# Attention and MLP for one decoded token: the load of wq divided between two DMA queues, 16 partitions on ScalarE's and 112 on SyncE's

## The chip, the cores and the metric

The kernel runs on one core of a Trainium2 chip. The metric is the device time of one execution in microseconds (us). The chip's core has a TensorE for matrix products (PE in the profile), a VectorE (DVE), a ScalarE (ACT), a GpSimd (POOL) and a SyncE (SP). Data come from HBM through 16 DMA engines, which are handed their work through queues: one that SyncE issues to (q1 in the profile) and one that ScalarE issues to (q10).

## What is computed

One token x of 512 numbers goes through a layernorm, attention over a cache of 16,384 keys and values with 8 key heads and 32 query heads, a projection with a residual, and then a second block: layernorm, a mixer, layernorm, an MLP with 1,792 hidden units. Cut to what matters:

```python
q = layernorm(x) @ wq                      # wq: 512 x 4096, bf16, 4 MB
scores = q . k_cache * 128 ** -0.5         # k_cache: 8 heads x 16384 x 128
o = softmax(scores) . v_cache              # v_cache: the same size
h = x + o @ wo                             # wo: 4096 x 512
# block B on layernorm(h): with a sequence of one, the mixer's four
# shifted parts are all zero, so that x1 is its input
out = h + x1 + gelu(layernorm(x1) @ w3) @ w4
```

The keys are 32 MB and the values 32 MB; wq, wo, w3 and w4 add 12 MB (wq and wo 4 MB each, w3 and w4 1.8 MB each). Each byte is used once.

## The kernel before

The kernel is written out by hand. A small class `Program` keeps a list of operations for each engine, in the order in which the Python calls are made. Each operation names the keys that it reads (`r`) and writes (`w`), and the class adds a wait on a semaphore wherever an operation needs one from another engine. An engine takes its own list strictly in order; so does SyncE, whose list is almost only DMA issues. A wait stops everything behind it on that engine.

**Loads.** `load` (L224-225) issues one DMA, by SyncE if nothing else is said. The order of issue is: x4, the small input of 1 KB, by ScalarE (L325); wq by SyncE (L326), 128 partitions of 32 KB each into the buffer `vb`; the first half and the second half of the first pair of key heads (L327-328), each 128 partitions of 32 KB, into the two halves of `kb`. The DMAs after that are issued when a buffer comes free: `vb` takes the values of pair 0 (8 MB, 64 KB in each partition, L241) when the matmuls on wq are done with it, and so on. The four pairs of heads follow each other; keys of the next pair are issued while the values of this one are still moving. At the end wo, w3 and w4 are loaded in pieces into the buffer of the keys.

**Head of the kernel.** VectorE makes an identity and from it `quarter` (L337). TensorE spreads x4 over all partitions with it (L339), VectorE makes sums, variance and inverse root of the layernorm (L272-L320) and writes `xn` (L345), then some constants and masks (L350-L370). TensorE multiplies `xn` with wq (L378, 32 matmuls), VectorE lays the queries out (L382, L388). The values of pair 0 are issued when the last of the matmuls of L378 is done.

**Loop over pairs.** For each half of the keys VectorE transposes (L397), TensorE makes scores (L405); then softmax (L416-L433), values (L448), gathering (L459-L465). After the loop come wo (L509), the second layernorm, w3 (L543), gelu (L555), w4 (L571) and the output (L577, L580).

Buffers that a load is to overwrite are guarded by keys: wq and the values of every pair share the key `"v"`, so that the load of the values waits for the readers of wq.

Of the kernel before, what the change touches and what calls it, by code (L numbers as in the profile page):

```python
# [110 lines left out]
HQ = 32  # L111
HKV = 8
SK = 16384
DH = 128
REP = HQ // HKV
FM = 1792
NCH = D // 128
FQ = FM // 4
NHC = FM // 128
WO = ((0, 24), (24, 32))  # L120
W3 = ((0, 4),)
W4 = ((0, 10), (10, 13), (13, 14))
# [10 lines left out]
def bass_sequential_preLN__gqa_block_cached__mixer_s_mlp__decode_kernel(  # L133
# [13 lines left out]
    with ExitStack() as ctx:  # L147
# [31 lines left out]
        xn = sb("xn", [128, NCH], BF16)  # L179
# [24 lines left out]
        hT = sb("hT", [128, NCH, 32], FP32)  # L204
        hcol = sb("hcol", [128, NHC, 32], BF16)
        fin = sb("fin", [64, 256], BF16)
        kb_all = sb("kb", [128, 256 * DH], BF16)
        kb = [kb_all[:, i * 128 * DH:(i + 1) * 128 * DH] for i in range(2)]
        vb = sb("vb", [128, 256 * DH], BF16)
        kt = sb("kt", [128, 128 * DH], BF16)  # L210
        wq_sb, wo_sb = vb, kb[0]
        w3_sb = kb[1][:, 0:NCH * FM].rearrange("p (k f) -> p k f", k=NCH)
        w4_sb = kb[1][:, NCH * FM:2 * NCH * FM].rearrange("p (m c) -> p m c", m=NHC)

# [9 lines left out]
        def load(name, dst, src, key, by="SP", also=()):  # L224
            P.op(by, lambda e: e.dma_start(dst, src), w=[key, *also], dma=name)  # L225

        def pair_rows(src, j):
            return src[0, 2 * j:2 * j + 2].rearrange("g (u t) d -> (g u) (t d)", u=64)

        def load_keys(j, y):  # L230
            n = 128 * DH
            if j in WHOLE:
                if y:
                    load("k0", kb_all[:, :], pair_rows(A_k_cache, j), ("r", 0, 0),
                         also=[("r", h, i) for h in range(2) for i in range(RPARTS)])
                return
            load(f"k{y}", kb[y][:, :], pair_rows(A_k_cache, j)[:, y * n:(y + 1) * n], ("r", y, 0),
                 also=[("r", y, i) for i in range(1, RPARTS)])

        def load_values(j):  # L240
            load("v", vb[:, :], pair_rows(A_v_cache, j), "v")  # L241


        def dve(fn, r=(), w=(), bank=()):
            return P.op("DVE", fn, r, w, bank)

        def act(fn, r=(), w=(), bank=()):
            return P.op("ACT", fn, r, w, bank)
# [4 lines left out]
        def pe(fn, r=(), w=(), bank=()):  # L253
            return P.op("PE", fn, r, w, bank)

        def piece(cuts, m):
            return [lo <= m < hi for lo, hi in cuts].index(True)

        def spin(n, out=1):

            for _ in range(n):
                pe(lambda e: e.matmul(O_ps[out][:, :], qb[:, 0, 0, 0:128], kt[:, 0:512], start=True, stop=True),  # L262
                   r=["qb", ("kt", 0)], w=[("O", out)], bank=[("O", out)])

        def copies(col, n):

            return col.to_broadcast([col.shape[0], n])
# [40 lines left out]
        def inverse_root(i, n, by):  # L308
# [7 lines left out]
            for k in range(3):  # L316
# [5 lines left out]
                   r=[(S, 8 + n), (T, n)], w=[key])  # L322


        load("x4", x4[:, :], A_x[0, 0:1, :].rearrange("o (q j) -> (o q) j", q=4), "x4", "ACT")  # L325
        load("wq", wq_sb[:, 0:NCH * HQ * DH], A_wq.rearrange("(p k) c -> p (k c)", k=NCH), "v")  # L326
        load_keys(0, 0)  # L327
        load_keys(0, 1)

# [8 lines left out]
            r=["ident_f"], w=["quarter"])  # L338
        pe(lambda e: e.matmul(O_ps[0][:, 0:128], quarter[:, :, :].rearrange("p q u -> p (q u)"), x4[:, :],  # L339
                              start=True, stop=True), r=["quarter", "x4"], w=[("O", 0)], bank=[("O", 0)])  # L340
# [6 lines left out]
            r=["hT", (("st", 0), 0), (("st", 0), 6)], w=["xn"])  # L347
# [9 lines left out]
            r=["ident_f"], w=["row32"])  # L357
        dve(lambda e: e.tensor_reduce(maskdd[:, :], ident_f[:, :].rearrange("p (n d) -> p d n", d=4), AX.X, ALU.add),
            r=["ident_f"], w=["maskdd"])
# [14 lines left out]
        for j, (row, key) in enumerate(rows):  # L374
            for k in range(NCH):
                for g in range(2):
                    at = k * HQ * DH + (2 * j + g) * REP * DH
                    pe(lambda e, row=row, k=k, g=g, at=at: e.matmul(  # L378
                        row[64 * g:64 * g + 64, :], copies(xn[:, k:k + 1], 64), wq_sb[:, at:at + REP * DH],
                        start=(k == 0), stop=(k == NCH - 1)), r=["xn", "v"], w=[key], bank=[key])  # L380
            for b in range(2):
                dve(lambda e, j=j, b=b, row=row: e.transpose(  # L382
                    qcol[:, j, 2 * REP * b:2 * REP * (b + 1), :].rearrange("p m u -> p (m u)"),
                    row.rearrange("p (h b i e) -> p b e h i", b=2, i=32, e=2)[:, b, :, :, :]),
                    r=[key], w=["qcol"], bank=[key])
        for a in range(4):
            lo, hi, at = 32 * a, 32 * a + 32, QPAD + 32 * a
# [65 lines left out]
        def gather(j):  # L453

            O, key = O_ps[j % 2], ("O", j % 2)
            for c in range(4):
# [10 lines left out]
               r=["od", "zo"], w=["A"], bank=["A"])  # L467

        load_values(0)
        for j in range(PAIRS):  # L470
            for y in range(2):
                transpose_keys(y, range(8))
                scores(j, y, range(8))
                if j < PAIRS - 1:
                    load_keys(j + 1, y)
            softmax(j)
            if j == PAIRS - 1:
                spin(SPINS[2], 0)
            values(j)
            if j == PAIRS - 1:  # L480
                spin(SPINS[3], 0)
            gather(j)
            if j < PAIRS - 1:
                load_values(j + 1)
        act(lambda e: e.activation(scr[0:1, 1:2], mean4[0:1, 0:1], ACTF.Gelu_apprx_tanh), r=["mean4"], w=["scr"])
        for n, (lo, hi) in enumerate(WO):
            load(f"wo{n}", wo_sb[:, lo * D:hi * D], A_wo.rearrange("(p r) c -> p (r c)", p=128)[:, lo * D:hi * D],
# [5 lines left out]
        for n, (lo, hi) in enumerate(W4):  # L493
# [7 lines left out]
            r=["o_m"], w=["o_f"])  # L501
# [3 lines left out]
        for r_ in range(32):  # L505
            q = r_ % 4
            if r_ == WO[1][0]:
                spin(SPINS[5])
            pe(lambda e, r_=r_, q=q: e.matmul(O_ps[0][32 * q:32 * q + 32, :], copies(o_b[:, r_:r_ + 1], 32),  # L509
                                              wo_sb[:, r_ * D:(r_ + 1) * D], start=(r_ < 4), stop=(r_ >= 28)),  # L510
               r=["o_b", ("r", 0, piece(WO, r_))], w=[("O", 0)], bank=[("O", 0)])
        h_ps, hkey = s_ps[:, 1, :], ("s", 1)
        pe(lambda e: e.matmul(h_ps[:, 0:128], quarter[:, :, :].rearrange("p q u -> p (q u)"), x4[:, :],
                              start=True, stop=False, skip_group_check=True),
           r=["quarter", "x4"], w=[hkey], bank=[hkey])
        dve(lambda e: e.tensor_copy(osum[:, :], O_ps[0][:, :]), r=[("O", 0)], w=["osum"], bank=[("O", 0)])  # L516
        for i in range(2):
            for n in range(2):
                pe(lambda e, i=i, n=n: e.matmul(
                    h2_ps[64 + 32 * i:96 + 32 * i, 128 * n:128 * n + 128], quarter[:, 2 * i + n, :], x4[:, :],  # L520
                    start=(n == 0), stop=False, skip_group_check=True), r=["quarter", "x4"], w=["h2"], bank=["h2"])
        spin(SPINS[6])
        for q in range(4):
            pe(lambda e, q=q: e.matmul(h_ps[32 * q:32 * q + 32, 0:128], copies(row32[:, 0:1], 32),
                                       osum[:, q * 128:(q + 1) * 128], start=False, stop=True, skip_group_check=True),
               r=["osum", "row32"], w=[hkey], bank=[hkey])
# [3 lines left out]
        for i in range(2):  # L530
            pe(lambda e, i=i: e.matmul(
                h2_ps[64 + 32 * i:96 + 32 * i, 0:256], copies(row32[:, 0:1], 32), osum[:, 256 * i:256 * i + 256],
                start=False, stop=True, skip_group_check=True), r=["osum", "row32"], w=["h2"], bank=["h2"])
        spin(SPINS[8])
        act(lambda e: e.activation(hc[:, :, :], hT[:, :, :], ACTF.Identity, bias=s[:, 0:1], scale=1.0),
            r=["hT", (S, 0)], w=["hc"])
        act(lambda e: e.activation(hr2[64:128, :], h2_ps[64:128, 0:256], ACTF.Identity, bias=0.0, scale=1.0),
            r=["h2"], w=["hr2"], bank=["h2"])


        for k in range(NCH):
            for q in range(4):
                pe(lambda e, k=k, q=q: e.matmul(s_ps[32 * q:32 * q + 32, 0, 0:FQ], hc[:, k, :],  # L543
                                                w3_sb[:, k, q * FQ:(q + 1) * FQ], start=(k == 0), stop=(k == NCH - 1)),
                   r=["hc", ("r", 1, piece(W3, k))], w=[("s", 0)], bank=[("s", 0)])
# [7 lines left out]
        for n in range(2):  # L553
            lo, hi = n * NHC // 2, (n + 1) * NHC // 2
            act(lambda e, lo=lo, hi=hi: e.activation(  # L555
                hg[:, :].rearrange("p (i m) -> p i m", m=NHC)[:, :, lo:hi],
                s_ps[:, 0, 0:FQ].rearrange("p (i m) -> p i m", m=NHC)[:, :, lo:hi],
                ACTF.Gelu_apprx_tanh, scale=s[:, 7:8]), r=[("s", 0), (S, 7)], w=[("hg", n)], bank=[("s", 0)])
            dve(lambda e, lo=lo, hi=hi: e.transpose(
                hcol[:, lo:hi, :].rearrange("p m u -> p (m u)"),  # L560
                hg[:, :].rearrange("p (i m) -> p m i", m=NHC)[:, lo:hi, :]), r=[("hg", n)], w=[("hcol", n)])
        dve(lambda e: e.tensor_tensor(xsum[64:128, :], hr2[64:128, :], xs2[64:128, :], ALU.add),
            r=["hr2", "xs2"], w=["xsum"])

        turns = {m: m % 2 if m < W4[0][1] else 0 for m in range(NHC)}
        for m in range(NHC):
            t = turns[m]
            same = [k for k in turns if turns[k] == t]
            bank, key = ((n_ps, "n"), (B_ps, "B"))[t]
            for o in range(2):  # L570
                pe(lambda e, m=m, o=o, lo=64 * t + 32 * o, bank=bank, same=same: e.matmul(  # L571
                    bank[lo:lo + 32, 0:256], hcol[:, m, :], w4_sb[:, m, o * 256:(o + 1) * 256],
                    start=(m == same[0]), stop=(m == same[-1])),
                   r=[("hcol", 2 * m // NHC), ("r", 1, 2 + piece(W4, m))], w=[key], bank=[("B" if t else "mn")])
        dve(lambda e: e.tensor_tensor(part[:, :], xsum[64:128, :], B_ps[64:128, 0:256], ALU.add),
            r=["B", "xsum"], w=["part"], bank=["B"])
        dve(lambda e: e.tensor_tensor(fin[:, :], part[:, :], n_ps[0:64, 0:256], ALU.add),  # L577
            r=["n", "part"], w=["fin"], bank=["mn"])
        for o, by in enumerate(("SP", "ACT")):
            P.op(by, lambda e, o=o: e.dma_start(out[0, 0:1, 256 * o:256 * o + 256], fin[32 * o:32 * o + 1, :]),  # L580
                 r=["fin"], w=[("out", o)], dma=f"out{o}")
# [32 lines left out]
```

## Time and profile before

| | us |
|---|---|
| median of 3 runs | 191.53 (191.33 to 191.57) |
| the profiled execution's own time | 191.19 |
| its span, from first to last instruction on the core | 189.9 |
| what lies around the span | 1.3 |
| PE, DVE, ACT, POOL busy | 122.6, 115.8, 9.4, 7.0 |
| moved through q1 (SyncE's queue) | 79.17 MB in 2,594 packets |
| moved through q10 (ScalarE's queue) | 10 packets, some 2 KB |

How to read it: the profile gives the busy time of each engine, a picture of the span in 40 slices, the DMA queues, the chain of work that ended last, and groups of instructions by line of the kernel. L378 is line 378 of the listing above. "SPq" and "ACTq" are DMA issues by SyncE and ScalarE: their time is that of the issue, not of the transfer. A packet is one piece of a DMA that one of the 16 DMA engines moves; the trace has start, duration, size and queue of each. The page's times are microseconds from the start of the span.

### The profile page before, as it was taken

The page shows a single profiled execution, that of the slowest core. Times are in us where ns is not written, and L with a number is a line of the kernel's source. Part 1 is how long each engine was busy: PE and PEld are TensorE (multiplying, and loading weights), DVE is VectorE, ACT ScalarE, POOL GpSimd, SP SyncE. Part 2 cuts the span into 40 slices and gives each one's busy share as a digit, 9 for nine tenths or more (in the row PEclk, how much of TensorE's full clock was granted, in tenths as well). Part 3 has the DMA queues.
Part 4 walks back from the last instruction along what each step waited for, and adds up shares of the span by engine and source line. Part 5 has one row for each costly group of instructions (what it writes and reads, how often), then busy time and mean ns, then how long its engine had stood idle before and what let it go on. Part 6 is the DMA issues. An engine that isn't in the chain of part 4 may idle for free.

```text
span 189.9 us, 1730 instructions
## 1 busy us (share of the span) xinstructions
PE 122.6 (65%) x726; PEld 45.9 (24%) x726; DVE 115.8 (61%) x176; ACT 9.4 (5%) x16; POOL 7.0 (4%) x15
## 2 busy tenths in 40 slices
PE   0129099693085004999449599944929998779893
PEld 0114033221032001342123222212313422334231
DVE  7755597993502007999450999935079897514274
ACT  3000000002000000000110000011000000500011
POOL 7100000000000000000000000000000000000032
PEclk9999969999558555799956999996575999999999
DMA  6999999999999999997999999999999999989992
GB/s 221 442 442 442 442 442 444 442 442 431 442 442 442 428 442 442 442 442 342 442 435 428 456 442 414 390 442 414 442 442 442 469 431 414 442 368 409 433 408 84
DMA packets 2610, 79.26 MB, mean 417 GB/s; under 512 B 298, under 2 KB 428, under 8 KB 556
## 3 DMA queue, kind: packets, MB, share of 16 engines
q1 hardware_dynamic: 2594, 79.17, 97.2%
q8 instruction: 5, 0.08, 0.2%
q14 instruction: 1, 0.01, 0.0%
q10 hardware_dynamic: 10, 0.00, 0.0%
HBM read 79.17 MB, written 0.00 MB: 417 GB/s over the span
## 4 chain that ended last, share of the span: by engine, by line
DMA 61%; DVE 31%; PE 4%; issue 1%; SPq 1%; ACT 1%; ACTq 0%
DMA kb<-in_A_k_cache_dram 46%; DVE kt L397 28%; DMA kb<-in_B_w_dram 14%; PE O_ps L448 3%; DVE pt L433 1%; SPq L225 1%; DVE mx L416 1%; ACT p_sb L429 1%; DVE od L462 1%; PE s_ps L405 1%; PE mn_ps L571 0%; DVE fin L577 0%; PE mn_ps L423 0%; PE mn_ps L419 0%; DVE od L459 0%
## 5 line engine op out<-in xcount | busy, mean ns | idle before, releaser
L405 PE MATMUL s_ps<-kt,qb 128*128 128x512 bf16 x256 | 69.5, 411 | 24.4 <-DVE kt L397 21.6
L397 DVE STREAM_TRANSPOSE kt<-kb 128x1024 int32<-128x1024 int32 x64 | 72.8, 1206 | 16.7 <-DMA kb<-in_A_k_cache_dram 16.7
L405 PEld LDWEIGHTS s_ps<-kt,qb 128*128 128x128 bf16 x256 | 22.8, 102 | 70.2 <-DVE kt L397 45.7
L448 PE MATMUL O_ps<-vb,pt 128*32 128x512 bf16 x256 | 21.9, 517 | 10.7 <-DMA vb<-in_A_v_cache_dram 6.3
L459 DVE TENSOR_SCALAR od<-O_ps,rowc 128x128 f32<-128x128 f32 x4 | 1.4, 350 | 28.0 <-PE O_ps L448 28.0
L448 PEld LDWEIGHTS O_ps<-vb,pt 128*32 128x32 bf16 x256 | 8.9, 125 | 22.5 <-issue 11.0
L433 DVE STREAM_TRANSPOSE pt<-p_sb 64x1024 bf16<-64x1024 bf16 x8 | 9.9, 1240 | 5.4 <-ACT p_sb L429 5.3
L262 PE MATMUL O_ps<-kt,qb 128*128 128x512 bf16 x52 | 12.9, 380 | 0.0
L429 ACT ACTIVATE p_sb<-s_ps,bias 128x1024 bf16<-128x1024 f32 x4 | 4.5, 1114 | 156.5 <-DVE nmh L425 156.5
L416 DVE TENSOR_REDUCE mx<-s_ps 128x1 f32<-128x1024 f32 x4 | 4.9, 1225 | 4.5 <-PE s_ps L405 4.5
L378 PE MATMUL O_ps<-vb,xn 128*64 128x512 bf16 x16 | 3.6, 631 | 5.8 <-DMA vb<-in_A_wq_dram 5.8
L315 POOL TENSOR_SCALAR st<-st 128x1 f32<-128x1 f32 x1 | 0.2, 244 | 177.5 <-DVE st L300 177.5
L262 PEld LDWEIGHTS O_ps<-kt,qb 128*128 128x128 bf16 x52 | 4.5, 99 | 6.0 <-issue 1.8
L465 PE MATMUL A_ps<-od,zz 128*128 128x128 f32 x8 | 2.0, 326 | 5.1 <-DVE od L462 5.1
L437 PE MATMUL A_ps<-acc,zz 128*128 128x1 f32 x8 | 1.6, 271 | 5.3 <-ACT p_sb L429 5.3
L462 DVE SCALAR_TENSOR_TENSOR od<-O_ps,rowc,od 128x128 f32<-128x128 f32 x12 | 4.2, 351 | 0.4
L419 PE MATMUL mn_ps<-ident_f,mx 128*1 128x128 f32 x8 | 1.5, 271 | 4.4 <-DVE mx L416 4.4
L337 DVE CAST quarter<-ident_f 4x128 bf16<-4x128 f32 x1 | 3.9, 3904 | 0.6 <-POOL ident_f L332 0.6
L339 PE MATMUL O_ps<-x,quarter 4*128 4x128 bf16 x1 | 0.3, 282 | 5.7 <-DVE quarter L337 5.7
L382 DVE STREAM_TRANSPOSE qcol<-O_ps 128x256 f32<-128x256 f32 x4 | 1.6, 428 | 3.9 <-PE O_ps L378 3.9
L378 PEld LDWEIGHTS O_ps<-vb,xn 128*64 128x64 bf16 x16 | 1.4, 167 | 7.2 <-DVE zz L367 5.9
L516 DVE COPY osum<-O_ps 128x512 f32<-128x512 f32 x1 | 0.7, 691 | 3.7 <-PE O_ps L509 3.7
(87 smaller groups left out, 50.9 us busy)
## 6 DMA issues: line engine op xcount, KB each, us to landing
kb<-in_A_k_cache_dram SPq DMA_DIRECT2D x6, 4096.0 KB, 23.5
vb<-in_A_wq_dram SPq DMA_DIRECT2D x1, 4096.0 KB, 12.2
kb<-in_A_wo_dram SPq DMA_DIRECT2D x1, 3072.0 KB, 27.2
kb<-in_B_w_dram SPq DMA_DIRECT2D x1, 1792.0 KB, 24.2
kb<-in_B_w_dram SPq DMA_DIRECT2D x1, 1280.0 KB, 27.0
kb<-in_A_wo_dram SPq DMA_DIRECT2D x1, 1024.0 KB, 29.2
kb<-in_B_w_dram SPq DMA_DIRECT2D x1, 384.0 KB, 27.4
kb<-in_B_w_dram SPq DMA_DIRECT2D x1, 128.0 KB, 27.3
```

The costliest lines, as they stand in the source:

```text
L225: P.op(by, lambda e: e.dma_start(dst, src), w=[key, *also], dma=name)
L262: pe(lambda e: e.matmul(O_ps[out][:, :], qb[:, 0, 0, 0:128], kt[:, 0:512], start=True, stop=True), r=["qb", ("kt", 0)], w=[("O", out)], ba ...
L337: dve(lambda e: e.tensor_copy(quarter[:, :, :], ident_f[0:4, 0:4].unsqueeze(2).to_broadcast([4, 4, 32])), r=["ident_f"], w=["quarter"])
L378: pe(lambda e, row=row, k=k, g=g, at=at: e.matmul(row[64 * g:64 * g + 64, :], copies(xn[:, k:k + 1], 64), wq_sb[:, at:at + REP * DH], star ...
L397: dve(lambda e, view=view: e.transpose(view(kt), view(kb[y])), r=[("r", y, n) for n in range(RPARTS)], w=[("kt", t)])
L405: pe(lambda e, n=n, c=c: e.matmul(s_ps[:, y, :], qb[:, n, j, QPAD - 4 * c:QW - 4 * c], ktv[:, n // 2, n % 2, :, 8 * c:8 * c + 8, :], start ...
L416: dve(lambda e: e.tensor_reduce(mx[:, :], s_all, AX.X, ALU.max), r=[("s", 0), ("s", 1)], w=["mx"], **both)
L429: act(lambda e: e.activation(p_sb[:, :], s_all, ACTF.Exp, bias=bias[:, 0:1], scale=float(SCALE), accum_out=acc[:, :]), r=[("s", 0), ("s", ...
L433: dve(lambda e, g=g: e.transpose(pt[64 * g:64 * g + 64, :, :, g, :], p_sb[64 * g:64 * g + 64, :]), r=["p"], w=["pt"])
L448: pe(lambda e, q=q, ct=ct, xl=xl, ch=ch: e.matmul(O_ps[j % 2][32 * ct:32 * ct + 32, :], pt[:, xl, ch, :, :].rearrange("p g u -> p (g u)"), ...
L462: dve(lambda e, block=block, c=c: e.scalar_tensor_tensor(od[:, :], block, rowc[:, c:c + 1], od[:, :], ALU.mult, ALU.add), r=[key, "rowc", ...
L465: pe(lambda e: e.matmul(A_ps[:, 0:128], zo[:, 96 - 32 * j:224 - 32 * j], od[:, :], start=False, stop=(j == PAIRS - 1), skip_group_check=True),
```

## The change

wq is loaded by two DMAs in place of one. Partitions 0 to 15 (512 KB) are issued by ScalarE as its first DMA, partitions 16 to 127 (3,584 KB) by SyncE as its first. x4 becomes ScalarE's second DMA; before, it was its only one until the output. The two parts have keys and semaphores of their own, `("wq", 0)` and `("wq", 1)`; the matmuls of L378 wait for both, and the loads of values name both among what they overwrite. Nothing else is touched; all lines behind the first edit move down by one to three.

```diff
+WQ = ((0, 16), (16, 128))
...
         def load_values(j):
-            load("v", vb[:, :], pair_rows(A_v_cache, j), "v")
+            load("v", vb[:, :], pair_rows(A_v_cache, j), "v", also=[("wq", 0), ("wq", 1)])
...
+        wq_in = A_wq.rearrange("(p k) c -> p (k c)", k=NCH)
+        for n, (lo, hi) in enumerate(WQ):
+            load(f"wq{n}", wq_sb[lo:hi, 0:NCH * HQ * DH], wq_in[lo:hi, :], ("wq", n), ("ACT", "SP")[n])
         load("x4", x4[:, :], A_x[0, 0:1, :].rearrange("o (q j) -> (o q) j", q=4), "x4", "ACT")
-        load("wq", wq_sb[:, 0:NCH * HQ * DH], A_wq.rearrange("(p k) c -> p (k c)", k=NCH), "v")
         load_keys(0, 0)
         load_keys(0, 1)
...
-                        start=(k == 0), stop=(k == NCH - 1)), r=["xn", "v"], w=[key], bank=[key])
+                        start=(k == 0), stop=(k == NCH - 1)), r=["xn", ("wq", 0), ("wq", 1)], w=[key], bank=[key])
```

## Prediction

> **What bounds the kernel now.** I read first the page's slices, then its DMA queues, then the chain of work that ended last, in order of time. The slices and queues:
>
> ```profile
> DMA  6999999999999999997999999999999999989992
> GB/s 221 442 442 442 442 442 444 442 442 431 442 442 442 428 442 442 442 442 342 442 435 428 456 442 414 390 442 414 442 442 442 469 431 414 442 368 409 433 408 84
> ...
> q1 hardware_dynamic: 2594, 79.17, 97.2%
> ...
> q10 hardware_dynamic: 10, 0.00, 0.0%
> ```
>
> The reader is to see that the 16 DMA engines are busy from the second slice to the 39th, and that one queue, SyncE's, holds them 97.2% of the span. The trace's packets say it more sharply. One packet is one partition's row; a row of 32 KB takes an engine 1.213 us in the steady stream (27.0 GB/s), the next starts where it ends, and from 2.6 to 186 us the engines together lack only 0.37 us (the mean over the 16) of being always in a packet of data. No engine takes over another's rows: each DMA of 128 partitions ends with 16 signs of completion, one per engine, and an engine that is late stays late to the end. In the last DMA (the end of w4) ten engines are done at 186.0 to 186.5 us and six at 187.2 to 187.8 us; those six have had one fetch of instructions each (page: q8 five, q14 one) among their rows.
>
> The chain, first and last pieces:
>
> ```profile
> 1.64 31.49 DMA kb<-in_A_k_cache_dram
> ...
> 42.34 30.01 DMA kb<-in_A_k_cache_dram
> ...
> 72.38 18.15 DVE kt L397 x16
> ...
> 160.02 27.42 DMA kb<-in_B_w_dram
> 187.44 0.04 issue
> 187.48 0.64 PE mn_ps L571 x8
> ```
>
> The DVE pieces in it lie beside full queues; the stream of rows runs on under them. So what makes the stream later in its first 13 us makes the end later by as much, on the slowest engine, and what makes it earlier makes the end earlier. Whatever delays only an engine's computing in the head costs something only if it outlasts its cover. The head:
>
> ```profile
> 0.71 0.56 ACTq L225 DMA_DIRECT2D x<-in_A_x_dram  x1
> 0.72 0.40 SPq L225 DMA_DIRECT2D vb<-in_A_wq_dram  x1
> ...
> 1.31 1.28 ACT L351 ACT_TABLE_LOAD   x1 [1.31 <-PEq L599]
> ...
> 5.66 0.28 PE L339 MATMUL O_ps<-x,quarter 4*128 4x128 bf16 x1 [5.66 <-DVE quarter L337]
> ...
> 10.06 0.29 DVE L345 TENSOR_SCALAR xn<-hT,st 128x4 bf16<-128x4 f32 x1
> ...
> 13.09 3.62 PE L378 MATMUL O_ps<-vb,xn 128*64 128x512 bf16 x16 [5.84 <-DMA vb<-in_A_wq_dram]
> ...
> 18.88 0.33 SPq L225 DMA_DIRECT2D vb<-in_A_v_cache_dram  x1
> ```
>
> Both queues are issued to at the same moment. By the packets, x4's first row starts at 1.67 us, wq's first rows at 1.74 to 2.04 us on fifteen engines and at 2.60 us on the last. These first rows take 1.54 to 2.19 us, not 1.21, and end at 3.57 to 4.14 us; from there the pace is steady, and wq is complete at 12.96 us.
>
> **The change part by part.**
>
> Bytes: the same. x4 (4 partitions) shows as 4 rows and 4 signs on q10, one row to an engine; I take it that 16 partitions give each engine one row and 112 give it seven, so 8 rows of wq per engine as before, 8 x 1.213 = 9.7 us.
>
> Change-over between queues: this is the term that I think decides. Before, an engine draws all rows of wq from one queue; after, from two. The trace shows what a foreign packet costs an engine's stream. Five fetches on q8 (16 KB, 0.61 us at 27.0 GB/s) took 0.95 to 1.07 us, 0.34 to 0.46 too much, and the row behind each of them took 0.48 to 0.55 us too long (2.90 for 2.42, 1.76 for 1.21, 0.79 for 0.31). The one late fetch on q14 took its normal 0.31, and the row behind it 0.61 too long. No data packet ran beside them on the same engine: the row begins where the fetch ends. Going out and back thus cost 0.83 to 0.96 us beyond the bytes for the five and 0.61 for the one; I take 0.93, near the middle of the five. ScalarE's row of wq is one such packet in SyncE's stream, on all 16 engines, the late six included, so it goes whole to the end. Lower bound: -0.57 us, the spread of the first rows' ends, if the change-over is free and all engines start like the first. Upper bound by change-overs: the completion sign behind the row is one more packet of ScalarE's, so twice 0.93 = 1.9 us. On the four engines with x4 it is up to 3.7 us (x4's row and sign are two more), from which up to 1.3 us is hidden where an engine isn't one of the six. I keep one change out and back, since q1's own signs (9 ns each) stretch no row.
>
> x4: before, its rows land at 1.7 us and are needed at 5.66, when `quarter` is ready. After, they stand behind a 32 KB row in the same queue. With one row of each queue ahead they land near 4.1 + 0.5 + 1.2 = 5.8 us, or 0.2 late. At worst they come behind all rows of wq, at 13.9. Then `xn` comes 4.7 us later (5.66 to 10.35) at 18.6 us, the queries' matmuls (13.09 to 18.81, 5.7) end at 24.3, and the values of pair 0 are issued at 24.4 us instead of 18.88. The two key halves keep q1 filled until 31.8 us on the first engine; so 7.4 us of cover remain. VectorE's key transposes (from 22.68) would begin some 3.4 us late, at 26.1 behind the queries' layout (1.8 us after the matmuls), and reach their second half 2.1 us late; the next keys, issued at 42.34, have cover until values 0 end at 51.2. Cost of x4: 0.
>
> ScalarE's table load at 1.31 waits behind one more issue (0.40 to 0.56); ScalarE is next needed at 46.1 us. Cost 0. SyncE's list has the same issues, one of them smaller. The second wait of L378 ends with the stream: wq comes at 12.96 + 0.93 = 13.9, and values 0 are issued at 19.8, with 12 us of cover. Cost 0 beyond the 0.93.
>
> Sum: 191.19 + 0.93 = 192.12 us for an execution like the profiled one. That one lies 0.34 below the median of the runs, 191.53; on the median **192.46 us**. All times below are on the median.
>
> **The rivals.**
>
> *The narrow part is slow to land* (slower, more). [...] Chance 0.26.
> [...]
>
> *The head starts better* (faster). Mechanism: 16 rows are described quicker than 128, so ScalarE's DMA fills the engine that now starts at 2.60 us as early as the others, and SyncE's rows stand ready behind. The last engine gains at most 2.60 - 1.74 = 0.86; I price it at the spread of the first rows' ends, 4.14 - 3.57 = 0.57: 190.96 us. It decides if a change-over between two queues that are both filled beforehand costs less than 0.57. For it: the fetches that I price from come unannounced into a running stream. Against it: the row that suffers is SyncE's, whose queue was full. Chance 0.22.
>
> *Nothing* (the rows of two queues follow like those of one, the start as before; SyncE's issue of wq, 0.40 us, is no shorter on the path, since the first rows come 0.6 us behind its end): 191.5. For it: q1's own DMAs follow each other without a gap. Against it: the stretched rows behind the fetches. Chance 0.15.
> [...]
>
> **How the numbers follow.** Forecast 0.37, its own range 191.8 (one change-over, 0.3) to 193.4 (two out and back); narrow part 0.26; better head 0.22; nothing 0.15. About 0.2%, or 0.38 us, is what a measurement of this kernel can tell from no change. Slower: 0.35 of the forecast and 0.26 = 0.61. Same: 0.15, 0.02 of the forecast, 0.04 of the better head = 0.21. Faster: 0.18. The range reaches from 190.9, below the better head's price, to 196.2, the narrow part with change-overs; outside are meetings of the 112 rows (about 0.12) and a gain above 0.6 us (about 0.06).
>
> **What would show it.** Right: first rows of q1 behind a q10 row longer by about 0.5 us, wq complete near 13.9, all later landings late by the same 0.9. [...] If the head is better, first rows end before 4.0 us on all engines and wq lands before 12.9. If q10's rows take 1.2 us and q1's rows aren't stretched, my price of the change-over is wrong. An L339 past 8 us with L378 waiting for VectorE would show the x4 path, which I hold free. If the end moves and wq's landing doesn't, my reading of the bound is wrong.

## The result and the profile after

The changed kernel takes 201.15 us (median of 6 runs, 200.89 to 201.50) where the kernel before takes 191.46 (6 runs beside it). The ratio is 1.0509, 95% interval 1.0495 to 1.0523: 5% slower, 9.7 us. The prediction said 192.46, with a range up to 196.2. The profiled execution has a span of 200.0 us, 10.1 more than before.

The slices and queues of the page after, and the issues of wq from the page's list (KB each, us from issue to landing):

```profile
DMA  9699899999999999999799999998999999979991
GB/s 203 111 295 223 315 426 446 452 454 433 423 419 419 433 485 472 446 419 433 331 433 419 459 459 433 433 436 387 433 426 446 524 436 419 419 339 426 414 411 65
...
q1 hardware_dynamic: 2578, 78.64, 95.2%
q10 hardware_dynamic: 42, 0.53, 2.0%
...
vb<-in_A_wq_dram SPq DMA_DIRECT2D x1, 3584.0 KB, 23.1
...
vb<-in_A_wq_dram ACTq DMA_DIRECT2D x1, 512.0 KB, 12.6
```

The reader is to read the two first lines together. The DMA engines are nearly as busy as before, but in slices 2 to 5 (5 to 25 us) they move 111 to 315 GB/s where they moved 442. So the engines don't wait for work: their packets last longer. From slice 6 on the two pages are alike. wq takes 23.1 us to land; the whole of it took 12.2.

The chain that ended last, in order of time, has the same pieces as before, most of them later by 9.6 to 10.1 us. The first piece is 41.62 us long instead of 31.49:

```profile
1.63 41.62 DMA kb<-in_A_k_cache_dram
...
52.47 29.49 DMA kb<-in_A_k_cache_dram
...
81.98 18.16 DVE kt L400 x16
...
169.73 27.80 DMA kb<-in_B_w_dram
197.53 0.04 issue
197.57 0.64 PE mn_ps L574 x8
```

And the timeline of the head (start, duration, engine, line, idle time before it and what ended it):

```profile
15.92 0.26 PE L342 MATMUL O_ps<-x,quarter 4*128 4x128 bf16 x1 [15.92 <-DMA x<-in_A_x_dram]
...
23.97 3.56 PE L381 MATMUL O_ps<-vb,xn 128*64 128x512 bf16 x16 [6.48 <-DMA vb<-in_A_wq_dram]
...
29.34 0.33 SPq L226 DMA_DIRECT2D vb<-in_A_v_cache_dram  x1
```

The matmul on x4 (L342) runs ten microseconds late, at 15.92 us instead of 5.66. Even so x4 isn't what the matmuls on wq (L381) wait for: they wait for wq.

What lasts longer shows in the trace's packets. The table gives the median duration of each engine's successive packets of 32 KB, 16 at a time:

| rows, in order | before | after |
|---|---|---|
| first of q1 | 1.95 us | 2.03 |
| ScalarE's row (q10) | – | 3.88 (3.29 to 4.37) |
| the next six of q1 | 1.21 each | 2.87, 1.72, 2.20, 2.22, 2.27, 2.10 |
| first row of the keys | 1.21 | 1.81 |
| all after that | 1.21 | 1.22 |

Taken over 1.213, the slow rows are worth 0.1 + 2.7 + 6.1 + 0.6 = 9.4 us on a middle engine. That is nearly the whole loss of 9.7. It has two parts: ScalarE's 16 rows, and, larger, the 112 rows of SyncE's that were expected to run at the old pace.

### The profile page after: what moved, and what is told of

It reads as the page before. It is cut to its first block, busy times and chain, and to the rows that moved or that the text cites. A ratio compares the mean times of both kernels' runs of the same rounds, so it can differ in the third digit from the quotient of the medians.

```text
span 200.0 us, 1728 instructions
## 1 busy us (share of the span) xinstructions
PE 124.7 (62%) x723; PEld 47.4 (24%) x726; DVE 115.8 (58%) x176; ACT 9.4 (5%) x16; POOL 7.0 (3%) x15
## 4 chain that ended last, share of the span: by engine, by line
DMA 63%; DVE 30%; PE 4%; SPq 1%; issue 1%; ACT 1%; ACTq 0%
DMA kb<-in_A_k_cache_dram 49%; DVE kt L400 27%; DMA kb<-in_B_w_dram 14%; PE O_ps L451 3%; DVE pt L436 1%; SPq L226 1%; DVE mx L419 1%; ACT p_sb L432 1%; DVE od L465 1%; PE s_ps L408 1%; PE mn_ps L574 0%; DVE fin L580 0%; PE mn_ps L426 0%; PE mn_ps L422 0%; DVE od L462 0%
## 5 line engine op out<-in xcount | busy, mean ns | idle before, releaser
L400 DVE STREAM_TRANSPOSE kt<-kb 128x1024 int32<-128x1024 int32 x64 | 72.8, 1206 | 15.8 <-DMA kb<-in_A_k_cache_dram 15.8
L408 PEld LDWEIGHTS s_ps<-kt,qb 128*128 128x128 bf16 x256 | 23.5, 104 | 68.6 <-DVE kt L400 42.4
L263 PE MATMUL O_ps<-kt,qb 128*128 128x512 bf16 x49 | 13.9, 419 | 0.4 <-issue 0.3
L342 PE MATMUL O_ps<-x,quarter 4*128 4x128 bf16 x1 | 0.3, 258 | 15.9 <-DMA x<-in_A_x_dram 15.9
L381 PE MATMUL O_ps<-vb,xn 128*64 128x512 bf16 x16 | 3.6, 624 | 6.5 <-DMA vb<-in_A_wq_dram 6.5
L263 PEld LDWEIGHTS O_ps<-kt,qb 128*128 128x128 bf16 x52 | 5.0, 108 | 7.2 <-issue 4.0
L342 PEld LDWEIGHTS O_ps<-x,quarter 4*128 4x128 bf16 x1 | 0.1, 99 | 15.9 <-issue 15.9
## 6 DMA issues: line engine op xcount, KB each, us to landing
vb<-in_A_wq_dram SPq DMA_DIRECT2D x1, 3584.0 KB, 23.1
```

What stands on the lines that cost most here:

```text
L381: pe(lambda e, row=row, k=k, g=g, at=at: e.matmul(row[64 * g:64 * g + 64, :], copies(xn[:, k:k + 1], 64), wq_sb[:, at:at + REP * DH], star ...
L400: dve(lambda e, view=view: e.transpose(view(kt), view(kb[y])), r=[("r", y, n) for n in range(RPARTS)], w=[("kt", t)])
L408: pe(lambda e, n=n, c=c: e.matmul(s_ps[:, y, :], qb[:, n, j, QPAD - 4 * c:QW - 4 * c], ktv[:, n // 2, n % 2, :, 8 * c:8 * c + 8, :], start ...
```

## The experiments

The theories. **A**: rows of different DMA engines that land in the same small group of partitions share that group's rate. **B**: two queues at work at once are slow. **C**: the change-over of the prediction. **D**: neighbouring rows are slow to read from HBM. Of A there are two forms: only the engines that meet wait (**A1**), or they hold up the others too (**A2**). Times of kernels with one timed execution are good to some tenths of a microsecond. "wq complete" is the last sign of completion of any of its parts; it is 12.96 us before and 23.83 after.

### Two queues, but all 128 partitions in each part

```diff
-WQ = ((0, 16), (16, 128))
+WQ = ((0, 2048), (2048, 16384))
-            load(f"wq{n}", wq_sb[lo:hi, 0:NCH * HQ * DH], wq_in[lo:hi, :], ("wq", n), ("ACT", "SP")[n])
+            load(f"wq{n}", wq_sb[:, lo:hi], wq_in[:, lo:hi], ("wq", n), ("ACT", "SP")[n])
```

> ScalarE and SyncE share wq as in the change, with the same bytes for each (512 KB and 3,584 KB), but each takes all 128 partitions: 4 KB of every partition on ScalarE's queue, 28 KB on SyncE's; x4 stays ScalarE's second. Theory A, landing in few partitions: the loss goes, wq is complete within 1 us of the 12.96 of before, and the time is within 1 us of before (191.5). Theory B, two queues at work at once: most of the 9.7 us stays, above 198. Theory C, change-over as in the prediction: between 0.3 and 1.9 us slower than before.

Measured: 191.53 us (11 runs) beside 191.41 (15 runs of before), ratio 1.0006, interval 0.9997 to 1.0015; wq complete at 13.3 us. The stages of the head in this kernel (per line: from:to, duration, busy time of each engine, granted clock, DMA share, GB/s):

```profile
2.00:6.00 4.00, 0.00 (x0) 0.00 (x0) 3.60 (x1) 1.25 (x2) 3.52 (x2) 1.00 0.73 294
6.00:12.00 6.00, 0.00 (x0) 0.00 (x0) 0.00 (x0) 0.00 (x0) 0.00 (x0) 1.00 1.02 436
12.00:22.00 10.00, 2.54 (x11) 1.31 (x13) 5.26 (x28) 0.00 (x0) 0.00 (x0) 1.00 1.02 438
```

and in the changed kernel:

```profile
2.00:6.00 4.00, 0.00 (x0) 0.00 (x0) 3.59 (x1) 1.25 (x2) 3.52 (x2) 1.00 1.06 156
6.00:12.00 6.00, 0.00 (x0) 0.00 (x0) 0.00 (x0) 0.00 (x0) 0.00 (x0) 1.00 0.79 175
12.00:22.00 10.00, 0.84 (x3) 0.60 (x3) 4.92 (x26) 0.00 (x0) 0.00 (x0) 1.00 1.07 262
```

The last column is the point: from 6 to 12 us 436 GB/s against 175, with the same bytes on the same queues. B falls, and so does C. The packets here are one of 28 KB (1.062 us) and one of 4 KB (0.159) by turns, 1.221 together where a row of 32 KB takes 1.213; eight turns out and back on each engine cost under 0.1 us. Also, first rows end at 3.42 to 4.12 us (before: 3.57 to 4.14), so nothing is won at the head either. x4 lands late here too (L342 runs at 15.58 us), with no loss in time.

### The change's two parts on one queue

```diff
-            load(f"wq{n}", ..., ("wq", n), ("ACT", "SP")[n])
+            load(f"wq{n}", ..., ("wq", n), "SP")
```

(and x4's load ahead of them.)

> The change's two parts, 16 and 112 partitions, both issued by SyncE on one queue; x4 is ScalarE's first DMA, as before. Theory A, few partitions: the 16 rows take 3 to 5 us each and the 112 rows about 2.2, the time stays within 2 us of 201.15. Theory B, two queues: rows of 1.21 us, time within 1 us of 191.5.

Measured: 200.85 us (4 runs), ratio 1.048, interval 1.0462 to 1.0499; wq complete at 22.66 us; the 16 rows take 3.82 (first rows, so some 0.7 of start in it), the 112 rows 1.7 to 2.8. The loss is in the cut by partitions, not in the queue.

### x4 first

> The change with x4 as ScalarE's first DMA and the 16 partitions as its second. If x4's lateness (L342 of the change ran at 15.92) costs nothing, the end stays within 1 us of 201.15, and L342 runs near 5.7. If it costs, the time comes 1 to 10 us nearer to before.

The edit moves x4's load ahead of the loop. Measured: 201.27 us. Its head:

```profile
5.65 0.28 PE L342 MATMUL O_ps<-x,quarter 4*128 4x128 bf16 x1 [5.65 <-DVE quarter L340]
...
24.31 3.28 PE L381 MATMUL O_ps<-vb,xn 128*64 128x512 bf16 x16 [17.06 <-DMA vb<-in_A_wq_dram]
```

L342 is back at its old place, and L381 starts as late as in the change (24.31 us against 23.97), still waiting for wq. x4's place costs nothing that this one run could tell.

### Where a row lands and where it is read from

Four kernels load wq with eight DMAs of 16 rows on SyncE's queue. The rows go to neighbouring partitions ("near") or to partitions 8 apart ("far"), and are read from neighbouring rows of wq or rows 8 apart. In the two mixed ones wq's rows lie in other partitions than the products expect.

```diff
-        for n, (lo, hi) in enumerate(WQ):
-            load(f"wq{n}", ...)
+        for n in range(8):
+            load(f"wq{n}", wq_sb[TO, 0:NCH * HQ * DH], wq_in[FROM, :], ("wq", n))
+        # near: 16 * n:16 * n + 16        far: n:128:8
```

> wq in eight DMAs of 16 rows on SyncE's queue, DMA n takes rows n, n+8, n+16, ... to the partitions of the same number. [...] Theory D (where rows are read, neighbours in HBM being slow together): 1.21 a row, wq near 13.

> Eight DMAs of 16 neighbouring rows to 16 neighbouring partitions. Both A and D expect slow rows as on ScalarE's queue of the change, 3 to 5 us; wq complete at 25 to 40. If the slow 16 rows were due to the second queue: 1.21 and 13.

> Eight DMAs of 16 neighbouring rows of wq to partitions 8 apart; wq's rows land in other partitions than the products expect, so the queries are others. Theory A: as to_far_from_far, to 0.3 us a row. Theory D: as to_near_from_near.

> Eight DMAs of rows 8 apart in wq to 16 neighbouring partitions; again rows land in other partitions than the products expect. Theory A: as to_near_from_near, to 0.3 us a row. Theory D: as to_far_from_far.

| to | from | time | wq complete | a row, steady |
|---|---|---|---|---|
| far | far | 201.83 us | 23.35 us | 2.55 us |
| far | near | 201.91 | 23.52 | 2.55 |
| near | near | 217.14 | 38.77 | 4.50 |
| near | far | 217.11 | 38.86 | 4.47 |

The mixed two in the stages where only wq moves, first to near from far, then to far from near:

```profile
6.00:36.00 30.00, 0.58 (x2) 0.50 (x2) 5.22 (x28) 0.00 (x0) 0.00 (x0) 1.00 0.93 108
```

```profile
6.00:20.00 14.00, 0.58 (x2) 0.50 (x2) 5.22 (x28) 0.00 (x0) 0.00 (x0) 1.00 1.07 220
```

Only the place of landing matters; D falls. The sizes fit, roughly, groups that take one engine's rate each. By the 1.213 us of a row, an estimate for 16 rows is 1.21 us through 16 groups, 2.43 through 8 and 4.85 through 4; measured are 1.21, 2.55 and 4.50, the last somewhat faster than that. As rates, 16 x 32 KB in 4.50 us is 117 GB/s for the near rows, and in 2.55 us 206 GB/s for the far ones. The groups are thus an estimate from these times; which partitions make a group isn't seen here.

### Other cuts

> wq in two parts of 64 partitions on SyncE's queue alone. Theory A in its simplest form (each group of 8 partitions that one engine serves now is a port with 27.0 GB/s, two engines meet in each of the 8 ports of a half): every row takes 2.43 us, 4 rows of each part, wq is complete near 21.5 and the time is near 201. If what matters is that a part isn't a power of two or doesn't start at partition 0: rows of 1.21, near 191.5.

Measured: 201.90 us, wq complete at 23.69 us, rows of 2.33 to 2.58 after the first, alike in both halves; near what A in its simplest form expected (2.43, with wq complete at 21.5), and close to the change in time.

> Both parts on SyncE's queue, cut at partition 112: 0 to 111 first, 112 to 127 second; x4 first on ScalarE. If a part's size matters and not where it starts, the 112 rows take 1.6 to 2.3 us as in the change, the 16 rows 4 to 4.5, and the time is within 1.5 us of 200.85.

Measured: 200.58 us, wq complete at 22.18 us. The 112 rows take 1.5 to 2.2 us in the middle (medians 1.88, 2.16, 2.24, 1.98, 1.48, 2.10, 2.18), the 16 rows 3.37 (2.58 to 4.12), shorter than the 4 to 4.5 expected; the row of keys behind each takes 2.86 in the middle in place of 1.21, so a part of the delay shows there. Where the cut lies hardly matters (200.58 to 201.90 us for four places), its kind does.

> Both parts on SyncE's queue, cut at partition 32. [...]

Measured: 201.43 us, wq complete at 22.91 us. The 32 rows take 2.56, which speaks for blocks of rows (engine e with rows 2e and 2e+1, two engines to a group by the estimate above; with rows e and e+16 the rows of a step would go to 16 neighbouring partitions, which took 4.50 in the near kernels). The 96 rows take 2.2 to 2.6 us on all 16 engines (the fastest row 2.20). From 6 to 18 us, most of it theirs, the core moves half of the 436 GB/s of wide parts:

```profile
6.00:18.00 12.00, 0.59 (x2) 0.50 (x2) 5.22 (x28) 0.00 (x0) 0.00 (x0) 1.00 1.01 218
```

None of them keeps 1.21. Which of the engines meet isn't seen here, so this run alone doesn't tell A1 from A2.

### The narrow part alone

wq as before, and beside it 16 rows that nobody needs, to partitions 0 to 15 of `kt`, as ScalarE's first DMA.

```diff
+        load("pr", kt[0:16, :], pair_rows(A_k_cache, 1)[0:16, 0:128 * DH], ("kt", 0), "ACT", ...)
```

> wq as before (128 partitions, SyncE), and beside it ScalarE's first DMA brings 16 rows of 32 KB, that nobody needs, to 16 neighbouring partitions of the buffer that the key transposes write later; x4 is ScalarE's second. It prices the narrow part alone: 512 KB more is 1.21 us a DMA engine, and four engines to a group of partitions (4.50 a row in the runs with 16 neighbouring partitions) is 3.3 more, so 191.5 + 1.2 + 2.5 to 3.5 = 195.2 to 196.2, if SyncE's rows beside them are 1.21. If SyncE's rows too are slowed while the 16 rows land: above 197.

Measured: 196.25 us beside 191.19 of before, 5.06 more: 1.21 for the bytes and 3.85 for the narrowness. The 16 rows take 3.63 in the middle (2.97 to 4.37). SyncE's row behind each of them is slowed too (2.43 in the middle, 1.62 to 3.05), and rows are at 1.21 to 1.22 from 9.55 us on, about when the 16 have landed (signs at 10.0 to 10.7). The expectation put slowed rows of SyncE's above 197 us. They came with 196.25, as the 16 rows themselves took less than the 4.50 that it reckoned with.

### Eight rows to neighbouring partitions, and to partitions four apart

wq as before; ScalarE brings, behind x4, four rows of 32 KB and four more, which the key transposes wait for.

```diff
+        for n, lo in enumerate((64, 96)):                    # neighbouring
+            load(f"pr{n}", kt[lo:lo + 4, :], pair_rows(A_k_cache, 1)[lo:lo + 4, 0:128 * DH], ("pr", n), "ACT")
...
+        for n, lo in enumerate((0, 32)):                     # four apart
+            load(f"pr{n}", kt[lo:lo + 16:4, :], pair_rows(A_k_cache, 1)[lo:lo + 16:4, 0:128 * DH], ("pr", n), "ACT")
```

> wq as before, and beside it ScalarE, after x4, brings 4 rows of 32 KB to partitions 64 to 67 and 4 more to 96 to 99 (rows that nobody needs; the key transposes wait for them). [...] Theory A2 (engines that meet hold up others): rows of 1.5 to 2.5 us on most engines while the 8 rows land.

> [...] If few groups of partitions are what held up all engines in the probe of partitions 64 to 67 and 96 to 99 (202.74), rows stay at 1.21 us on nearly all engines and the time is 191.2 + 2 x 1.21 = 193.6 at most. If a DMA on only four engines, or the second queue, held them up, it stays above 200.

Measured: to neighbouring partitions 202.74 us beside 191.19 (11.6 more), wq complete at 24.69; to partitions four apart 193.13 beside 191.6 (1.5 more), wq complete at 15.25. The stage in which the rows land, first neighbouring, then four apart:

```profile
2.00:6.00 4.00, 0.28 (x1) 0.10 (x1) 3.62 (x2) 1.43 (x2) 3.52 (x2) 1.00 0.76 303
6.00:12.00 6.00, 0.58 (x2) 0.50 (x2) 5.14 (x28) 0.00 (x0) 0.00 (x0) 1.00 1.08 169
```

```profile
2.00:6.00 4.00, 0.28 (x1) 0.10 (x1) 3.62 (x2) 1.49 (x2) 3.52 (x2) 1.00 0.76 311
6.00:12.00 6.00, 0.59 (x2) 0.50 (x2) 5.13 (x28) 0.00 (x0) 0.00 (x0) 1.00 1.00 431
```

Until 6 us the two are alike. Then, with as many bytes from the same queue, four rows to a DMA, the whole core moves 169 GB/s or 431. In the packets of the first probe all 12 rows of q1 that begin beside the first four take 2.88 to 4.98 us; from 12.5 us, about when the four have landed (signs from 12.67 us on), rows are at 1.21 again, and it happens once more with the second four. In the other probe q10's rows take 1.213 and so do q1's. By the estimate of a row's time for each group, rows that take 1.21 us sixteen at a time, as q1's do in before, go to sixteen different groups; so at most one of the 12 was bound for the group of the four, and the others were slow all the same. If the groups are right, this is A2: engines that write to one group hold up engines that write elsewhere. The two probes differ in two more things, which other runs above show not to matter: how far apart the rows are read from (a row takes 2.55 us in both far kernels, 4.50 and 4.47 in the near ones) and the half of the partitions (rows of 2.57 us in both halves of the cut at 64).

## Why the prediction was wrong

**What bounds the kernel: right.** The stream of rows sets the end. wq's delay of 10.9 us (12.96 to 23.83) comes out as 10.1 in the span; the six DMA engines late by fetches are there in both kernels.

**Change-over, +0.93: wrong, it is none.** "ScalarE's row of wq is one such packet in SyncE's stream" is the step that failed in the forecast's own term. Rows of two queues that are both filled follow each other at 1.221 us for 32 KB, eight times over, and rows of q10 in the probe with partitions four apart take their 1.213 and stretch nothing. So the stretched rows around a fetch of instructions don't carry over to rows of data; why a fetch stretches them, these runs don't show. With all partitions in each part, the ratio is 1.0006. That the forecast had the sign right (slower) is luck, since the cost that it came from isn't there.

**"I take it that 16 partitions give each engine one row and 112 give it seven ... 8 x 1.213 = 9.7 us": right in the count, wrong in the duration, and this is the step that cost most.** The rows are 16 and seven sets of 16 in the packets. But 1.213 us was read from DMAs of 128 partitions only, and was carried over to parts that land otherwise. Narrow rows can keep it: those of the probe with partitions four apart took 1.213 us too. In the change the 16 rows took 3.88 in the middle, and the sets of the 112 rows 1.7 to 2.9.

**The narrow part: right as a rival, and near in price.** It had a chance of 0.26. The upper end of the range, 196.2 for the narrow part with change-overs, leaves some 3.7 us for it above 191.53 + 0.93. No run shows the term behind that price; what they showed in its place is 3.85 us, with the part alone. The trace of before couldn't show a narrow load's rate (x4, its only narrow load, takes 15 ns a row). The near kernels come close to the 3.85: their 4.50 us a row is 3.7 times 1.213, so an estimate is four engines to a group, each waiting for the rows of three others, 3 x 1.213 = 3.64 us. But the delay doesn't fall on the narrow rows alone: with the part alone they took 3.63 and SyncE's rows behind them 2.43, 6.06 together, 3.63 more than two rows of 1.213. So the rows of the other queue don't fill gaps; they are held up as well. The forecast should have rested less on the one price that it could show.

**"meetings of the 112 rows (about 0.12)": this seems to be what happened**, and was left out of the range. What remains of the loss when the narrow part is taken off is 9.7 - 3.85 = 5.8 us. It wasn't priced. That the 112 rows go in blocks of seven is worked out from the cuts at 32 and 64, not seen; the trace doesn't give the DMA engine of a packet. Nor is it seen which of them meet. So the 5.8 may come from meetings and from their holding up everybody, as in the probe with neighbouring partitions (rows of 2.88 to 4.98 us); how it divides isn't shown. What the runs do show is the price of the 112 rows without the narrow part ahead of them: in the cut at 112 an engine's second to seventh row take an estimated 12.1 us by the medians above, 4.9 more than six rows of 1.213.

**The better head: wrong.** The last first row starts at 2.22 us instead of 2.60, as the rival had it (with both parts on one queue it is 2.08, so the second queue isn't shown to be the reason), but with all partitions in both parts wq isn't complete earlier (13.3, 12.96 before).

**x4, no cost: right**, though it lands later than the worst case of the text (13.9; it was 15.8). With x4 first the time is 201.27, and with x4 late and wide parts it is that of before. The chain of that wide kernel does lead through x4's landing; the stream of rows beneath it hides that:

```profile
1.13 14.31 DMA x<-in_A_x_dram
```

## What to carry to other kernels

In these runs a DMA's rate went with how its rows are dealt out to partitions, so cutting a load by partitions isn't free even when each part still uses all 16 DMA engines (201.15 us for 191.46); cut by columns, with all 128 partitions in each part, it went through two queues at no cost (191.53 for 191.41, and no gain). A duration read from a profile holds for the shape that it was read from: a row's 1.21 us belonged to loads of 128 partitions, and with 16 neighbouring ones it was 4.50. A DMA share near 1 with falling GB/s is the mark of this fault: from 12 to 22 us the changed kernel has a share of 1.07 at 262 GB/s, the one before 1.02 at 442. The engines look busy while their packets last longer.

## What the runs showed of the hardware that was not expected

Eight rows, 256 KB, to two sets of four neighbouring partitions cost 11.6 us, as much as some 5 MB at the full pace (11.6 us x 431 GB/s): while the first four rows landed, all 12 rows that began beside them on the other queue took 2.88 to 4.98 us instead of 1.21. As many rows to partitions four apart cost 1.5 us. How the rows that share a landing place reach the others isn't seen here.
